# Packed fp16 splits for every attention unit, and the low parts of w_in formed by TensorE

## The chip, the cores and the metric

The kernel runs on one core of one Trainium2 chip. The metric is the device time of one execution in microseconds (us); several runs are timed and their median is used. One further execution is recorded by the hardware profiler, and its trace is what the profile below shows.

The core's engines run side by side, each through its own queue in program order: TensorE (PE; its weight loads are listed as PEld), VectorE (DVE), ScalarE (ACT), GpSimd (POOL), and SyncE (SP), which issues the transfers between HBM and on-chip memory here.

## The reference

The kernel computes an attention layer with a short window and block summaries, followed by a two-layer MLP with GELU. There are 4 batches, 8 heads, 768 positions, 64 channels a head; the MLP goes from 512 to 2048 and back, for 3072 tokens. The two weight matrices arrive as float64.

```python
k_sum = k.reshape(B, H, nb, 32, D).max(axis=3)          # 24 blocks of 32 positions
v_sum = v.reshape(B, H, nb, 32, D).mean(axis=3)
scores_l = where(|i - j| < 16, q @ k.T / 8, -1e9)
scores_s = q @ k_sum.T / 8 + log(32)
a = softmax(concat([scores_l, scores_s]))
x = (a @ concat([v, v_sum]))                              # to [3072, 512]
h = x @ w_in                                              # [3072, 2048]
out = (0.5 * h * (1 + erf(h / sqrt(2)))) @ w_out          # [3072, 512]
```

## The kernel before

**Splits.** TensorE multiplies fp16 at one pass and fp32 in several. For fp32 accuracy an operand is split into two fp16 parts, `hi = fp16(x)` and `lo = fp16(x - hi)`, and a product is three fp16 matmuls: hi by hi, hi by lo, lo by hi.

**Weights.** Each matrix is fetched in 16 pieces of 128 x 512 numbers (`fetch_w_in i`, `fetch_w_out f`). Three integer instructions on VectorE (`wi_bits i 0` to `2`, lines L294 to L303) turn float64 bits into fp32 in a buffer `wst`, of which there are three. ScalarE casts the hi part (`wi_hi`, L310), VectorE subtracts it for the lo part (`wi_lo`, L324). A piece's raw bits land in the later space of the `gh` and `gl` tiles or in a `stage` buffer.

**Attention.** The work is cut into 24 units of 4 heads by 256 queries (4 blocks of 64). For a block of 64 queries, 128 keys stand on the partitions: 64 of the window, 24 block maxima, 8 zeros, 32 of the window. A unit's steps are `load_q`, `load_k`, `load_v`, `load_vs`, then `k_hi`, `q_hi` (casts on GpSimd), `k_lo`, `q_lo` (VectorE), `scores` (TensorE, to `pss`), `add_mask` (VectorE, to `s32`), `maximum` (GpSimd, over the partitions), `shift` (VectorE), `exponent` (ScalarE), `p_hi` (GpSimd), `p_lo` (VectorE), `v_hi` (ScalarE), `v_lo` (VectorE), `values` (TensorE, to `psv`; columns of ones in v give the denominators), the norm (`norm_den` to `norm_mult`), and `x_hi`, `x_lo`. In the scores 64 rows of k's hi part and 64 rows of its lo part fill the 128 rows of the array, against q held twice, so that two matmuls (with q's hi and with its lo) make the product; q takes 1024 columns on 128 partitions, k 1280 on 64.

Units 0 to 3 (`NF = 4`, `self.fp`) take another way: mask, scores, shift and values are fp32 matmuls on data that is not split (`f_mask` L543, `scores_f` L576, `f_shift` L551 and L552, `values` L648).

**MLP.** A chunk c is 256 tokens, two units. `phase1 c i` makes 256 of the 2048 hidden columns: 24 matmuls of 256 columns (L708 to L710) into a `psh` buffer, of which there are two; it reads the w_in pieces 2i and 2i + 1. `gelu`, `g_hi` (ScalarE) and `g_lo` (VectorE) follow, over `g32` (three buffers). `phase2 c i` is 12 matmuls of 512 columns (L742 to L744) into `pso`, `store` and `put` bring a half chunk out.

**Order.** No scheduler runs: `ORDER`, a list of steps written out in the source, is walked once and each step issues its instructions, so each engine's queue and SyncE's queue of transfers have the order of that list.

Of the kernel before, what the change touches and what calls it, by code (L numbers as in the profile page):

```python
# [52 lines left out]
fill_v 0, load_k 0, fetch_vt 0, fill_v 1, fetch_k 0 1, load_mask, load_q 0, fetch_k 0 2, load_k 1, load_ind,
fetch_vt 2, prep_k 0 1, fetch_k 0 3, load_q 1, prep_k 0 2, fetch_k 0 0, fetch_w_in 10, f_mask 0, fetch_vt 1,
prep_k 0 3, load_v 0, sum_vt 0, prep_k_end 0 1, kf_sums 1, prep_k 0 0, k_sums 0 1, fetch_w_in 0, prep_k_end 0 0,
kf_sums 0, scores 0, wi_bits 10 0, fetch_w_in 4, k_sums 0 0, wi_bits 10 1, wi_bits 10 2, fetch_w_in 14, wi_hi 10,
wi_lo 10, fetch_w_in 7, sum_vt 1, f_evac 0, load_k 2, wi_bits 0 0, maximum 0, wi_bits 0 1, sum_vt 2, load_v 1,
wi_bits 0 2, wi_bits 4 0, wi_hi 0, wi_bits 4 1, f_mask 1, mean_vt, wi_bits 4 2, fetch_w_in 1, wi_lo 0, wi_hi 4,
scores 1, wi_bits 7 0, fetch_w_in 9, wi_lo 4, wi_bits 7 1, kf_sums 2, wi_bits 7 2, fetch_w_in 3, load_vs 0,
wi_bits 14 0, wi_hi 7, wi_bits 14 1, fetch_w_in 2, f_evac 1, load_vs 1, wi_lo 7, wi_bits 14 2, f_shift 0,  # L60
fetch_w_in 6, maximum 1, wi_bits 1 0, wi_hi 14, wi_bits 1 1, fetch_w_in 11, wi_bits 1 2, wi_bits 9 0, wi_hi 1,
wi_bits 9 1, fetch_w_in 8, exponent 0, wi_bits 9 2, wi_lo 1, load_q 2, wi_lo 14, fetch_w_in 5, wi_hi 9, f_shift 1,
wi_bits 3 0, wi_bits 2 0, wi_bits 2 1, fetch_w_in 12, wi_bits 2 2, wi_bits 3 1, wi_hi 2, load_k 3, wi_bits 3 2,
values 0, exponent 1, wi_lo 2, fetch_w_in 15, wi_lo 9, wi_hi 3, wi_lo 3, load_q 3, wi_bits 8 0, fetch_w_in 13,
wi_bits 5 0, wi_bits 5 1, f_mask 2, norm_den 0, wi_bits 5 2, load_v 2, wi_bits 6 0, wi_hi 5, wi_bits 8 1, scores 2,
kf_sums 3, norm_take 0, norm_rec 0, load_k 4, wi_lo 5, norm_spread 0, norm_mult 0, f_evac 2, wi_bits 6 1, values 1,
wi_bits 8 2, x_hi 0, maximum 2, wi_bits 6 2, wi_hi 8, x_lo 0, wi_hi 6, wi_lo 8, load_k 5, wi_lo 6, f_mask 3,
norm_den 1, load_v 3, wi_bits 11 0, load_vs 2, shift 2, k_hi 4, scores 3, norm_take 1, exponent 2, load_q 4,
norm_rec 1, k_hi 5, norm_spread 1, norm_mult 1, load_vs 3, load_v 4, wi_bits 11 1, x_hi 1, values 2, wi_bits 11 2,
f_evac 3, q_hi 4, x_lo 1, wi_hi 11, wi_bits 12 0, maximum 3, wi_lo 11, wi_bits 12 1, load_v 5, wi_bits 12 2,  # L70
phase1 0 0, norm_den 2, wi_bits 15 0, fetch_w_out 0, wi_bits 15 1, wi_bits 15 2, load_vs 4, wi_hi 12, norm_take 2,
wi_hi 15, fetch_w_out 6, phase1 0 1, norm_rec 2, gelu 0 0, norm_spread 2, load_vs 5, norm_mult 2, g_hi 0 0, wi_lo 12,
phase1 0 2, x_hi 2, g_lo 0 0, gelu 0 1, x_lo 2, g_hi 0 1, v_hi 4, wi_lo 15, phase1 0 3, shift 3, gelu 0 2, g_hi 0 2,
wi_bits 13 0, load_q 5, exponent 3, wi_bits 13 1, phase1 0 7, wo_bits 0 0, wo_bits 0 1, wi_bits 13 2, gelu 0 3,
wo_bits 6 0, fetch_w_out 10, wo_bits 6 1, values 3, wo_bits 6 2, wi_hi 13, g_hi 0 3, wi_lo 13, wo_hi 6, wo_bits 0 2,
v_hi 5, g_lo 0 2, fetch_w_out 1, fetch_w_out 2, wo_hi 0, g_lo 0 1, phase1 0 6, norm_den 3, wo_lo 6, wo_lo 0, gelu 0 7,
norm_take 3, g_hi 0 7, norm_rec 3, phase1 0 4, norm_spread 3, gelu 0 6, wo_bits 1 0, g_hi 0 6, norm_mult 3,
phase1 0 5, wo_bits 2 0, x_hi 3, wo_bits 1 1, x_lo 3, wo_bits 1 2, wo_bits 2 1, wo_hi 1, wo_bits 2 2, wo_lo 1,
wo_hi 2, g_lo 0 3, wo_lo 2, gelu 0 5, wo_bits 10 0, g_hi 0 5, g_lo 0 7, g_lo 0 5, gelu 0 4, g_lo 0 6, g_hi 0 4,
phase1 1 1, wo_bits 10 1, wo_bits 10 2, k_lo 4, wo_hi 10, fetch_w_out 3, fetch_w_out 4, fetch_w_out 11, wo_lo 10,  # L80
q_lo 4, load_k 6, phase1 1 2, gelu 1 1, g_lo 0 4, g_hi 1 1, wo_bits 3 0, wo_bits 3 1, wo_bits 3 2, phase1 1 3,
gelu 1 2, wo_bits 4 0, fetch_w_out 5, wo_hi 3, wo_bits 4 1, g_hi 1 2, wo_lo 3, wo_bits 4 2, phase1 1 0, gelu 1 3,
wo_bits 11 0, fetch_w_out 7, g_hi 1 3, wo_bits 11 1, wo_hi 4, wo_bits 11 2, wo_lo 4, wo_hi 11, fetch_w_out 13,
phase1 1 5, wo_bits 5 0, wo_bits 5 1, wo_bits 5 2, wo_bits 7 0, wo_hi 5, fetch_w_out 9, scores 4, wo_bits 7 1,
phase2 0 0, wo_lo 5, q_hi 5, wo_bits 7 2, k_hi 6, wo_lo 11, wo_hi 7, fetch_w_out 8, g_lo 1 1, phase2 0 1,
wo_bits 13 0, gelu 1 0, wo_bits 13 1, g_hi 1 0, wo_bits 13 2, g_lo 1 0, wo_hi 13, fetch_w_out 12, phase1 1 4, wo_lo 7,
wo_bits 9 0, wo_bits 9 1, wo_lo 13, phase2 0 2, wo_bits 8 0, wo_bits 8 1, wo_bits 9 2, wo_bits 8 2, wo_hi 9,
fetch_w_out 14, phase2 0 3, wo_bits 12 0, wo_hi 8, fetch_w_out 15, wo_lo 9, wo_lo 8, g_lo 1 3, phase2 0 5,
wo_bits 12 1, wo_bits 12 2, wo_bits 14 0, wo_hi 12, fetch_k 1 1, wo_bits 14 1, phase2 0 4, wo_bits 15 0, wo_bits 15 1,
wo_bits 14 2, wo_bits 15 2, wo_hi 14, fetch_k 1 2, wo_lo 12, wo_hi 15, fetch_k 1 0, wo_lo 14, wo_lo 15, add_mask 4,  # L90
phase2 0 7, g_lo 1 2, maximum 4, k_lo 6, gelu 1 5, g_hi 1 5, phase2 0 6, gelu 1 4, k_lo 5, g_hi 1 4, store 0 1,
g_lo 1 4, load_k 7, phase1 1 7, put 0 1, shift 4, q_lo 5, exponent 4, load_q 6, phase1 1 6, g_lo 1 5, load_k 8,
v_lo 4, gelu 1 7, p_hi 4, prep_k 1 1, load_v 6, scores 5, p_lo 4, fetch_k 1 3, gelu 1 6, q_hi 6, g_hi 1 6, add_mask 5,
values 4, g_hi 1 7, k_hi 7, store 0 0, g_lo 1 7, put 0 0, phase2 1 1, norm_den 4, maximum 5, q_lo 6, norm_take 4,
prep_k 1 0, phase2 1 3, g_lo 1 6, shift 5, phase2 1 5, v_lo 5, exponent 5, load_q 7, k_lo 7, load_v 7, phase2 1 0,
p_hi 5, prep_k_end 1 0, load_k 9, norm_rec 4, k_sums 1 0, p_lo 5, phase2 1 2, norm_spread 4, norm_mult 4, prep_k 1 2,
x_hi 4, values 5, x_lo 4, fetch_v 1 0, fetch_v 1 1, prep_k 1 3, scores 6, norm_den 5, prep_k_end 1 1, fetch_v 1 3,
phase2 1 7, q_hi 7, add_mask 6, k_sums 1 1, k_hi 8, norm_take 5, phase2 1 4, maximum 6, store 1 1, norm_rec 5,
norm_spread 5, put 1 1, norm_mult 5, q_lo 7, phase2 1 6, x_hi 5, shift 6, x_lo 5, scores 7, exponent 6, load_q 8,
prep_v 1 0, phase1 2 2, store 1 0, k_hi 9, add_mask 7, put 1 0, fetch_v 1 2, p_hi 6, prep_v 1 1, phase1 2 1, gelu 2 2,  # L100
maximum 7, p_lo 6, fetch_k 2 2, k_lo 8, g_hi 2 2, phase1 2 0, gelu 2 1, g_lo 2 2, g_hi 2 1, load_k 10, q_hi 8,
prep_v 1 2, prep_v 1 3, phase1 2 3, gelu 2 0, g_hi 2 0, shift 7, load_vs 6, g_lo 2 0, phase1 2 4, exponent 7,
load_vs 7, q_lo 8, g_lo 2 1, load_q 9, gelu 2 3, p_hi 7, scores 8, fetch_k 2 3, k_lo 9, fetch_k 2 1, phase2 2 1,
k_hi 10, p_lo 7, v_hi 6, load_k 11, v_hi 7, v_lo 6, phase2 2 0, q_hi 9, gelu 2 4, v_lo 7, load_v 8, g_hi 2 4,
g_hi 2 3, add_mask 8, values 6, g_lo 2 3, maximum 8, q_lo 9, phase1 2 6, norm_den 6, load_vs 8, g_lo 2 4, norm_take 6,
norm_rec 6, load_v 9, norm_spread 6, phase1 2 5, gelu 2 6, norm_mult 6, g_hi 2 6, shift 8, v_hi 8, values 7, x_hi 6,
g_lo 2 6, load_q 10, exponent 8, load_vs 9, phase2 2 3, x_lo 6, v_lo 8, k_lo 10, norm_den 7, load_v 10, p_hi 8,
phase2 2 2, gelu 2 5, prep_k 2 3, load_k 12, norm_take 7, norm_rec 7, phase1 2 7, v_hi 9, norm_spread 7, norm_mult 7,
load_vs 10, g_hi 2 5, g_lo 2 5, x_hi 7, scores 9, p_lo 8, gelu 2 7, g_hi 2 7, phase2 2 4, q_hi 10, x_lo 7, k_hi 11,
add_mask 9, v_lo 9, phase1 3 0, maximum 9, g_lo 2 7, load_v 11, q_lo 10, phase1 3 2, gelu 3 0, k_lo 11, g_hi 3 0,  # L110
shift 9, load_k 13, phase1 3 5, gelu 3 2, load_vs 11, g_hi 3 2, g_lo 3 0, exponent 9, g_lo 3 2, load_q 11, prep_k 2 1,
# [742 lines left out]
```

## Time and profile before

| what | us |
|---|---|
| median of 3 runs (680.51 to 684.58) | 683.58 |
| the profiled execution's own time | 686.86 |
| its span, first to last instruction | 684.8 |
| PE busy | 638.6 (93%) |
| DVE busy | 472.6 (69%) |
| ACT busy | 297.0 (43%) |
| POOL busy | 172.7 (25%) |

A page of the profile gives busy time by engine, the span in 40 slices (each digit a busy share in tenths; PEclk the clock that TensorE was granted), and groups of instructions by line. A group's row reads: line, engine, operation, out<-in by the program's tile names, sizes, count | busy us, mean ns of one | idle time of the engine just before them, and who ended it. Matmuls are pipelined, so their listed durations overlap; what one costs is the distance from its start to the next one's start. Other views used are the chain of work that ended last in order of time, the busy time of each engine in chosen stretches, the waits (who waited for whom), and the timeline.

### The profile page before, as it was taken

What the parts mean: (1) busy time and instruction counts of PE and PEld (TensorE: products, weight loads), DVE (VectorE), ACT (ScalarE), POOL (GpSimd) and SP (SyncE); (2) the same over time, 40 slices, a digit from 0 to 9 for tenths busy, and PEclk for the clock granted to TensorE, in tenths of its full rate; (3) what the DMA queues carried; (4) which work ended last, traced back from release to release, by engine and by line L of the source; (5) the groups of instructions that cost most, each with busy time, mean ns of one, the idle gap of its engine ahead of it and who ended that gap; (6) DMA issues with size and microseconds to landing.
All of it is one profiled execution on the core that took longest, in us unless ns stands there. A gap on an engine that the chain in (4) does not pass through costs nothing.

```text
span 684.8 us, 12436 instructions
## 1 busy us (share of the span) xinstructions
PE 638.6 (93%) x5356; PEld 444.2 (65%) x5356; DVE 472.6 (69%) x581; ACT 297.0 (43%) x419; POOL 172.7 (25%) x103
## 2 busy tenths in 40 slices
PE   1989999889898799999899989999999899999997
...
DVE  1784778999999998948889986628318974146210
...
PEclk9855569999999999999999999999999999999999
...
GB/s 247 378 218 199 139 66 125 149 180 152 162 117 141 167 91 225 180 57 72 91 127 79 88 77 53 133 1 111 45 16 66 84 69 16 1 32 1 16 16 32
DMA packets 26998, 72.24 MB, mean 105 GB/s; under 512 B 3008, under 2 KB 6720, under 8 KB 26944
## 3 DMA queue, kind: packets, MB, share of 16 engines
...
q8 instruction: 42, 0.69, 0.4%
...
## 4 chain that ended last, share of the span: by engine, by line
PE 66%; DVE 25%; issue 3%; DMA 2%; ACT 2%; POOL 1%; SPq 1%; DVEq 0%; ACTq 0%; POOLq 0%
PE psh L708 9%; PE psh L709 9%; PE psh L710 9%; PE pso L743 8%; PE pso L742 8%; PE pso L744 8%; PE psv L648 4%; DVE ql L568 3%; DVE gl L728 3%; PE pss L576 3%; DVE k L562 2%; DVE s L607 2%; DVE s L593 2%; PE pss L543 2%; DVE v_lo L634 2%
## 5 line engine op out<-in xcount | busy, mean ns | idle before, releaser
L708 PE MATMUL psh<-xh,w_in_h 128*128 128x256 f16 x768 | 210.4, 274 | 6.4 <-ACT g L715 6.4
L709 PE MATMUL psh<-xl,w_in_h 128*128 128x256 f16 x768 | 210.3, 274 | 0.5 <-DVE xl L698 0.5
L710 PE MATMUL psh<-xh,w_in_l 128*128 128x256 f16 x768 | 210.4, 274 | 0.0
L728 DVE SCALAR_TENSOR_TENSOR gl<-g,gh 128x512 f16<-128x512 f32 x96 | 76.7, 804 | 106.9 <-ACT gh L724 106.3
L743 PE MATMUL pso<-w_out_l,gh 128*128 128x512 f16 x384 | 146.4, 381 | 0.5 <-DVE w_out_l L324 0.5
L742 PE MATMUL pso<-w_out_h,gh 128*128 128x512 f16 x384 | 146.5, 382 | 0.0
L744 PE MATMUL pso<-w_out_h,gl 128*128 128x512 f16 x384 | 146.0, 380 | 0.0
L602 POOL PARTITION_ALL_REDUCE q<-s x24 | 82.5, 3439 | 95.9 <-ACT s L547 55.1
L715 ACT ACTIVATE g<-psh 128x512 f32<-128x512 f32 x96 | 56.9, 595 | 109.8 <-PE psh L710 107.9
L559 POOL CAST qh<-q 128x1024 f16<-128x1024 f32 x20 | 25.6, 1278 | 268.7 <-PE pss L589 254.7
L709 PEld LDWEIGHTS <-w_in_h 128*128 128x128 f16 x768 | 75.6, 98 | 18.8 <-issue 7.3
L708 PEld LDWEIGHTS <-w_in_h 128*128 128x128 f16 x768 | 75.7, 99 | 11.9
L710 PEld LDWEIGHTS <-w_in_l 128*128 128x128 f16 x768 | 75.5, 98 | 10.0 <-issue 0.9
L744 PEld LDWEIGHTS <-gl 128*128 128x128 f16 x384 | 37.8, 98 | 46.6 <-issue 1.9
L742 PEld LDWEIGHTS <-gh 128*128 128x128 f16 x384 | 37.8, 99 | 41.0 <-issue 0.8
L743 PEld LDWEIGHTS <-gh 128*128 128x128 f16 x384 | 37.8, 98 | 40.7 <-issue 0.5
L724 ACT ACTIVATE gh<-g 128x512 f16<-128x512 f32 x96 | 59.9, 629 | 2.7
L617 POOL CAST ph<-s 128x1024 f16<-128x1024 f32 x20 | 27.2, 1359 | 68.0 <-ACT s L613 68.0
L613 ACT ACTIVATE s<-s 128x1024 f32<-128x1024 f32 x22 | 23.3, 1057 | 48.5 <-DVE s L607 48.4
L651 PE MATMUL psv<-pl,v_hi 128*128 128x64 f16 x320 | 32.9, 199 | 7.6 <-DVE pl L621 7.6
L568 DVE TENSOR_TENSOR ql<-q,qh 128x1024 f16<-128x1024 f32 x20 | 39.3, 1966 | 0.1
L650 PE MATMUL psv<-ph,v_hi 128*128 128x64 f16 x320 | 33.2, 199 | 6.3 <-DVE den L680 5.9
...
## 6 DMA issues: line engine op xcount, KB each, us to landing
...
```

Source lines behind the costliest of these rows:

```text
L568: nc.vector.tensor_tensor(out=self.ql, in0=self.q32, in1=self.qh, op=ALU.subtract)
L602: nc.gpsimd.partition_all_reduce(out_ap=self.m32, in_ap=self.s32, channels=P, reduce_op=bass_isa.ReduceOp.max)
L650: nc.tensor.matmul(self.psv[:, sl], vh[:, vo : vo + P], self.ph[:, sl], start=True, stop=False)
L708: nc.tensor.matmul(ph[:, e, :], w_in_h[:, k, fs], xh[:, k, :], start=(k == 0), stop=False)
L709: nc.tensor.matmul(ph[:, e, :], w_in_h[:, k, fs], xl[:, k, :], start=False, stop=False)
L710: nc.tensor.matmul(ph[:, e, :], w_in_l[:, k, fs], xh[:, k, :], start=False, stop=(k == NCC - 1))
L715: nc.scalar.activation(g32, pht.pop((c, i)), AF.Gelu, scale=1.0 / (SC_X * SC_WI))
L724: nc.scalar.activation(gh, g32t[c, i], AF.Copy, scale=SC_G)
L728: nc.vector.scalar_tensor_tensor(out=gl, in0=g32t.pop((c, i)), scalar=SC_G, in1=gh, op0=ALU.mult, op1=ALU.subtract)
L742: nc.tensor.matmul(p, gh[:, f, js], w_out_h[:, f, :], start=(f == 0), stop=False)
L743: nc.tensor.matmul(p, gh[:, f, js], w_out_l[:, f, :], start=False, stop=False)
L744: nc.tensor.matmul(p, gl[:, f, js], w_out_h[:, f, :], start=False, stop=(f == NFC - 1))
```

## The change

1. The fp32 way of units 0 to 3 is removed, with its inputs `kf` and `vf`, the masks by matmul and the shift by matmul. All 24 units use the split path.
2. q and k are packed: two heads of a pair on the upper and the lower 64 partitions. q takes 512 columns on 128 partitions (before 1024, held twice), k 640 (before 1280 on 64). k's hi and lo parts have tiles of their own, `k_hi` and `k_lo`, in place of `k16`.
3. The scores become 48 matmuls of 64 columns on 64 rows each (before 32 on 128 rows): three products, each for the lower half of the rows (`e = 0`) and the upper half (`e = 1`) in turn, the halves to different PSUM banks.
4. The maximum goes to a tile of its own, `m32` (one buffer), not over `q32`.
5. Each w_in piece gets a `wi_diff`: TensorE forms 128 times the fp32 piece minus the hi part in a `psh` buffer (one fp32 matmul and one fp16 matmul), and ScalarE evacuates it as the lo part (`wi_lo`). w_out keeps its lo parts on VectorE.
6. `prep_k_end` writes one packed hi and lo of the block maxima (two VectorE instructions instead of five), and `k_sums` copies both with ScalarE.
7. `qh` and `ql` get two buffers each instead of one, `g32` five instead of three.
8. `ORDER` is a new list. Pieces 2, 0, 3, 1 of w_in come first and the first `phase1` stands behind 17 of the 48 `wi_bits` (before: 42).

Steps ahead of `phase1 3 0` in the two lists, where they differ or matter here:

| step | before | after |
|---|---|---|
| phase1, phase2, values, norms | 24, 21, 8, 8 | 24, 21, 8, 8 |
| scores, add_mask, shift | 10, 6, 7 | 9, 9, 9 |
| k_lo, q_lo | 7, 6 | 11, 11 |
| v_lo, p_lo | 6, 5 | 10, 8 |
| prep_k, prep_k_end | 9, 4 | 11, 5 |
| maximum | 9 | 9 |
| wi_lo on VectorE | 16 | 0 |
| wi_diff | 0 | 16 |
| wi_bits, wo_bits, wo_lo, g_lo | 48, 48, 16, 23 | 48, 48, 16, 23 |

The new list around the first `phase1`:

```diff
+load_vs 3, norm_mult 1, k_hi 5, v_hi 3, add_mask 3, q_hi 5, x_hi 1, wi_bits 4 2, x_lo 1, wi_hi 4, fetch_w_in 8,
+wi_bits 5 1, phase1 0 0, wi_bits 5 2, wi_bits 6 0, wi_hi 5, fetch_w_in 9, wi_bits 6 1, shift 2, wi_bits 6 2,
+exponent 2, maximum 3, v_lo 3, fetch_w_in 10, wi_hi 6, phase1 0 1, gelu 0 0, v_lo 2, k_lo 4, load_v 4, p_hi 2,
+g_hi 0 0, wi_diff 4, shift 3, load_k 6, gelu 0 1, wi_lo 4, wi_diff 5, wi_bits 7 0, exponent 3, wi_bits 7 1, wi_diff 6,
...
```

The core of the rest:

```diff
-    NQ16, NG32, NOT = 1, 3, 1
+    NQ16, NG32, NOT = 2, 5, 1
...
     def prep_k_end(b, g):
...
+        hi, lo = ks16[b, g][:, 0], ks16[b, g][:, 1]
+        nc.vector.tensor_copy(out=hi, in_=ks32[b][:, rs])
+        nc.vector.tensor_tensor(out=lo, in0=ks32[b][:, rs], in1=hi, op=ALU.subtract)
...
         def load_q(self):
-            self.q32 = ld.tile([P, UCOLS], F32, tag="q32", name=f"q32_{self.nm}")
-            rows = slice(0, D if self.fp else P)
-            nc.sync.dma_start(out=self.q32[rows], in_=qd[self.u, rows])
+            self.q32 = ld.tile([P, QCOLS], F32, tag="q32", name=f"q32_{self.nm}")
+            nc.sync.dma_start(out=self.q32, in_=qd[self.u])
...
+        def k_hi(self):
+            nc.gpsimd.tensor_copy(out=self.kh[:, :, 0:TQ], in_=self.k32)
...
+        def k_lo(self):
+            nc.vector.tensor_tensor(out=self.kl[:, :, 0:TQ], in0=self.k32, in1=self.kh[:, :, 0:TQ], op=ALU.subtract)
...
         def scores(self):
-            if self.fp:
-                return self.scores_f()
...
-                    nc.tensor.matmul(self.pss[:, sl], kf[:, kb : kb + P], self.qh[:, sl], start=True, stop=False)
-                    nc.tensor.matmul(self.pss[:, sl], kf[:, kb : kb + P], self.ql[:, sl], start=False, stop=True)
+            for i in range(NR * CT):
+                kb = (i // CT * (CT + 1) + i % CT) * KW
+                sl = slice(i * TQ, (i + 1) * TQ)
+                for n, (k, q) in enumerate(((kh, self.qh), (kh, self.ql), (kl, self.qh))):
+                    for e in range(2):
+                        rows = slice(e * D, (e + 1) * D)
+                        nc.tensor.matmul(
+                            self.pss[:, e * QCOLS + i * TQ : e * QCOLS + (i + 1) * TQ], k[rows, kb : kb + P], q[rows, sl],
+                            start=(n == 0 and not masked), stop=(n == 2 and (i == NR * CT - 1 or not masked)),
+                        )
...
         def maximum(self):
-            self.m32 = self.q32
+            self.m32 = wk.tile([P, UCOLS], F32, tag="m32", bufs=1, name=f"m32_{self.nm}")
```

`wi_diff i` and `load_neg` stood in the source before, uncalled; the new list calls them. `eye` is 128 times the identity, `neg` minus the identity in fp16:

```python
def weight_diff(key, dst_h):
    ps = diffs[key] = ps_h.tile([P, 2, CH], F32, tag="psh", name=f"psw_{key}")
    flat = ps.rearrange("p e j -> p (e j)")
    nc.tensor.matmul(flat, eye, raws[key], start=True, stop=False)
    nc.tensor.matmul(flat, neg, dst_h, start=False, stop=True)
```

and `weight_lo`, where such a difference exists, evacuates it on ScalarE: `nc.scalar.activation(dst_l, flat.rearrange(...), AF.Copy)`.

More of the change, by code (lines that the diff above doesn't have):

```diff
@@ L49 @@
 UPB = len(UNITS) // B
-NF = 4
 ORDER = '''
[L53 to L111, printed above, removed]
-phase1 3 1, prep_k 2 2, gelu 3 5, p_hi 9, prep_k_end 2 1, fetch_k 2 0, fetch_v 2 2, fetch_v 2 0, p_lo 9, phase2 2 6,
@@ new lines @@
+phase2 0 5, add_mask 4, k_hi 6, q_hi 6, wo_lo 12, maximum 4, g_lo 1 2, phase2 0 6, k_lo 5, q_lo 5, load_k 7, g_lo 1 1,
+load_q 7, v_lo 4, gelu 1 5, scores 5, g_hi 1 5, phase2 0 7, shift 4, store 0 0, load_v 6, put 0 0, add_mask 5,
+exponent 4, k_hi 7, q_hi 7, g_lo 1 3, phase2 1 0, maximum 5, g_lo 1 4, v_lo 5, gelu 1 7, phase2 1 2, prep_k 1 1,
+load_v 7, g_hi 1 7, g_lo 1 5, p_hi 4, store 0 1, shift 5, put 0 1, phase2 1 1, p_lo 4, exponent 5, prep_k 1 0,
+prep_k_end 1 0, phase2 1 3, fetch_k 1 2, p_hi 5, k_lo 7, k_sums 1 0, k_lo 6, p_lo 5, load_k 8, values 4, q_lo 6,
```

398 lines of the change are left out of this document (199 added, 199 removed).

## The prediction

> **What bounds the kernel now.** I read the page's slices first, then the chain of work that ended last over the first 100 us, then busy time by stretch.
>
> ```profile
> PE   1989999889898799999899989999999899999997
> DVE  1784778999999998948889986628318974146210
> PEclk9855569999999999999999999999999999999999
> ```
>
> One digit is 17.1 us. PE looks full nearly throughout, but from the third to the sixth slice its granted clock is 0.5 to 0.6, and VectorE (DVE) is full from there to slice 15 only. So there are three stages. The chain, in order of time (start us, us, what), tells what the first one is:
>
> ```profile
> 25.49 6.25 PE pso_vt L440 x8
> ...
> 38.28 2.07 PE pss L551 x2
> ...
> 55.62 7.02 PE psv L648 x32
> ...
> 87.65 7.02 PE psv L648 x32
> ```
>
> These are the fp32 matmuls of units 0 to 3: the shift by the maximum (L551 and, alike, L552; 1.0 us a record), the scores (L576), the values (L648, 7.02/32 = 0.22 us a record of 64 columns; an fp32 matmul has two records). They run one behind another at half clock until the first `phase1` can start. The stretches show the second stage:
>
> ```profile
> 0.00:95.00 95.00, 78.34 (x271) 51.43 (x272) 57.88 (x84) 24.70 (x39) 27.92 (x26) 0.68 0.68 218
> 95.00:120.00 25.00, 25.00 (x213) 22.01 (x212) 20.64 (x35) 20.30 (x29) 0.00 (x0) 0.92 0.34 109
> 120.00:250.00 130.00, 113.94 (x1036) 77.37 (x1034) 127.83 (x158) 60.52 (x85) 42.95 (x23) 0.97 0.49 149
> 250.00:685.00 435.00, 421.29 (x3844) 293.40 (x3841) 266.29 (x307) 191.46 (x267) 101.86 (x55) 1.00 0.22 68
> ```
>
> Columns: length, then busy PE, weight loads, DVE, ACT, POOL, then clock, DMA share, GB/s. From 120 to 250 us DVE is busy 127.83 of 130 and PE idles 16: DVE bounds. After 250 us PE is busy 421 of 435, and DVE 266: PE bounds, at full clock.
>
> The boundary falls on a step that makes a good ruler, `phase1 3 0`. Ahead of it, in both order lists, stand the same 24 `phase1`, 21 `phase2` and 8 `values`. In the trace it starts at 249.74:
>
> ```profile
> 249.53 0.38 PE L744 MATMUL pso<-w_out_h,gl 128*128 128x512 f16 x1
> 249.74 0.27 PE L708 MATMUL psh<-xh,w_in_h 128*128 128x256 f16 x1
> 249.85 0.27 PE L709 MATMUL psh<-xl,w_in_h 128*128 128x256 f16 x1
> ```
>
> One phase2 matmul takes 0.21 us start to start, one of phase1 0.11. The span is thus 249.7 us to the ruler plus 435.1 behind it (684.8). Ahead of the ruler DVE is busy 57.88 + 20.64 + 127.83 less the last 0.26, so 206.1 us, and idle 43.6. The sum needs four terms: DVE's work ahead, DVE's idle ahead, PE's work behind, stalls behind.
>
> **Term 1, DVE's work ahead of the ruler.** VectorE's groups in the first 250 us (count, busy us, mean ns):
>
> ```profile
> L562 DVE TENSOR_TENSOR k<-k,k 64x1280 f16<-64x1280 f32 x7 | 14.2, 2032 | 0.2
> L324 DVE SCALAR_TENSOR_TENSOR w_in_l<-wst_i,w_in_h 128x512 f16<-128x512 f32 x16 | 12.3, 784 | 17.4 <-ACT w_in_h L310 17.3
> L634 DVE SCALAR_TENSOR_TENSOR v_lo<-v,v_hi 128x512 f16<-128x512 f32 x11 | 11.3, 1069 | 0.0
> L607 DVE TENSOR_TENSOR s<-s,q 128x1024 f32<-128x1024 f32 x7 | 9.6, 1366 | 0.0
> L568 DVE TENSOR_TENSOR ql<-q,qh 128x1024 f16<-128x1024 f32 x6 | 9.0, 1498 | 0.0
> L621 DVE TENSOR_TENSOR pl<-s,ph 128x1024 f16<-128x1024 f32 x5 | 8.7, 1735 | 0.0
> L593 DVE SCALAR_TENSOR_TENSOR s<-mask_sb,pss 128x1024 f32<-128x1024 f32 x6 | 7.3, 1216 | 0.1
> L405 DVE TENSOR_REDUCE ks<-kp 128x24 f32<-128x768 f32 x5 | 4.7, 939 | 0.1
> L419 DVE TENSOR_TENSOR ksum<-ks,ks 64x48 f16<-64x48 f32 x8 | 2.6, 329 | 0.1
> L418 DVE COPY ksum<-ks 64x48 f16<-64x48 f16 x8 | 2.2, 280 | 0.3
> L680 DVE TENSOR_TENSOR den<-psv,dent 64x512 f32<-64x512 f32 x8 | 5.6, 694 | 0.1
> L414 DVE CAST ks<-ks 128x48 f16<-128x48 f32 x4 | 0.7, 187 | 0.1
> L303 DVE SCALAR_TENSOR_TENSOR wst_o<-wraw,wst_o 128x512 int32<-128x512 int32 x16 | 11.6, 733 | 0.3
> ```
>
> Counts are those of the two order lists ahead of the ruler; the packed tiles have half the columns, so I take half a row.
> - `wi_lo` leaves DVE: 16 x 0.784 = -12.5.
> - `k_lo`: 7 x 2.032 becomes 11 x 1.016: -3.0. `q_lo`: 6 x 1.498 becomes 11 x 0.749: -0.8.
> - `prep_k_end`: 4 x (0.187 + 2 x 0.280 + 2 x 0.329) becomes 5 x (0.187 + 0.329): -3.0.
> - Units 0 to 3 now use the split path. `add_mask` 6 to 9: +3.6. `shift` 7 to 9: +2.7. `v_lo` 6 to 10, two instructions each: +8.6. `p_lo` 5 to 8: +5.2. `prep_k` 9 to 11: +1.9.
>
> Sum +2.7: 208.8 us. The change takes no DVE work from the stage that DVE bounds; it gives back all it saves.
>
> **Term 2, DVE's idle time ahead of the ruler**, 43.6 us now. Who it waited for in the first 250 us (us, times, longest):
>
> ```profile
> DVE w_in_l L324 <- ACT w_in_h L310: 17.3, 5, 7.4
> DVE ks L405 <- DMA gl<-in_kp_dram: 12.2, 2, 8.3
> DVE dent L663 <- ACT den L659: 3.9, 4, 3.0
> DVE ks L405 <- DMA gh<-in_kp_dram: 3.0, 1, 3.0
> ```
>
> The 17.3 us stand on `wi_lo`, which DVE no longer has; behind them ACT, in order, was held by PE's fp32 scores. Both go. The k blocks (8.3 us to the first, 6.9 for the later ones) are fetched first instead of third, and unit 0's q and k right behind them: I take 6.5 to the first and 1 more. New waits: a unit's chain (scores, mask, maximum, shift, exponent, `p_hi`) has steps on PE, POOL and ACT, of which one is long:
>
> ```profile
> L602 POOL PARTITION_ALL_REDUCE q<-s x24 | 82.5, 3439 | 95.9 <-ACT s L547 55.1 <-DVE s L593 37.3 <-issue 3.4
> ```
>
> DVE has the integer steps of `w_in` to lay between, but none before the first piece has landed, so unit 0 and 1 cost about 7, and I leave 5.5 for the rest, nearest to the 6.6 us that it idles from 95 to 250 now. Together 20. The ends are 12 (start and a third of the rest) and 43.6 (as now). The ruler then starts at 208.8 + 20 = 228.8 instead of 249.7: -20.9.
>
> **Is PE ready for that?** Ahead of the first `phase1` the new list has, for DVE, 17 integer steps of 0.73, four each of `prep_k`, `k_lo`, `q_lo` and `add_mask`, two each of `shift`, `p_lo` and `v_lo` (38.6 us by the rows), and for each of two units the norm with `x_lo`, six instructions at most like L680's 0.69 (8.3): 47 us. With the 14.5 us of idle that lie early it starts near 62 instead of behind the last L648 of the chain, at 94.7. PE's work from there to the ruler: 24 phase1 of 24 x 0.11 = 63, 21 phase2 of 12 x 0.21 = 53, six `values` and five `scores` of 1.4 to 1.7 each, 16, and twelve `wi_diff`. One of these is two fp32 records of 512 columns, at most 6.25/8 = 0.78 each by the chain's row at mixed clock, and an fp16 one of 0.21: 1.8 x 12 = 21. Together 153 in 167 us: hidden. If that cover were gone they would cost their 21. `wi_lo` on ACT adds 16 evacuations of `psh`, of which one takes
>
> ```profile
> L715 ACT ACTIVATE g<-psh 128x512 f32<-128x512 f32 x24 | 14.1, 594 | 8.3 <-PE psh L710 6.7 <-DVE gl L728 1.5
> ```
>
> 0.6 us, to an engine busy 45 of its first 120 us: hidden, 9.5 us if not. GpSimd's casts of q and k halve, and nine maxima stay nine. The single `m32` buffer makes a maximum wait for the shift before it; on SyncE's queue `q32` comes free at `q_lo` already, and q's loads halve where DMA is not the limit (share 0.22 behind the ruler). I cost these at nothing; without cover each would show as one maximum, 3.4 us, where the next unit is late.
>
> **Term 3, PE's work behind the ruler.** 72 phase1, 75 phase2 and 16 values stand there in both lists; scores are 14 and 15. A unit's scores now, first and last matmul and what follows:
>
> ```profile
> 137.40 0.19 PE L588 MATMUL pss<-qh,k 128*128 128x64 f16 x1
> 137.43 0.19 PE L589 MATMUL pss<-ql,k 128*128 128x64 f16 x1
> 138.30 0.19 PE L589 MATMUL pss<-ql,k 128*128 128x64 f16 x1
> 138.33 0.38 PE L742 MATMUL pso<-w_out_h,gh 128*128 128x512 f16 x1
> ```
>
> 32 in 0.93 us: 0.029 each. After the change there are 48, on 64 rows each, upper and lower half in turn. No row shows two halves at once. Bounds: 0.029 each as they come (1.39), or 0.029 a pair if the halves run together (0.70). I take the single one, the nearest row in type and width. And changing between 64 and 128 rows has a price that the fp32 scores show:
>
> ```profile
> 24.65 0.84 PE L576 MATMUL pss<-q,w_out_h 64*128 64x64 f32 x3
> 25.08 0.42 PE L576 MATMUL pss<-q,w_out_h 64*128 64x64 f32 x1
> 25.43 1.15 PE L440 MATMUL pso_vt<-vt,ind_sb 128*88 128x512 f32 x1
> ```
>
> Three starts to 25.08 are 0.215 apart, the next, on 128 rows, comes 0.35 later: 0.135 lost. The Trainium skill, "TensorEngine Tiling (Array Packing)", section Key Properties, says that changing the tiling mode drains the engine while changing the tile alone does not; the row agrees with the first half, and no row here shows the second. Twice 0.135 a unit: 15 x (1.39 + 0.27) - 14 x 0.93 = +11.9. In pairs it would be 15 x (0.70 + 0.27) - 14 x 0.93 = +1.5.
>
> **Term 4, stalls behind the ruler.** PE idles 13.7 of 435 us there, the tail among it. DVE's work behind the ruler falls by 24 us (13 `k_lo` by 1.016 each, and `q_lo` from 14 x 1.498 to 13 x 0.749), so its late results, which are what PE waits for, come earlier: I take -4; ends 0 and -9.
>
> **Sum:** -20.9 + 11.9 - 4 = -13.0. Against the profiled execution, 686.86 us (span 684.8 and 2.1 around it): 673.9. That execution lies 3.3 above the median of the three runs shown, 683.58, to which the comparison will be made: 670.6, so 671.
>
> **The rivals.**
> - The halves run in pairs: term 3 is +1.5, the time 660. For it: two halves write different PSUM banks and alternate. Against: each matmul here already starts every 0.029 us with a weight load of its own, so the start may be the limit and not the columns. Chance 0.28. The Trainium skill, "TensorE: Matmul & The Clock Gate", Part 3, has matmuls on different row groups run at once; by that rule this case comes out. Its Part 1 has no two starts closer than about 25 ns, and by that figure term 3 would be an estimated +9.0. No row here shows either.
> - Idle moves instead of going. `wst` has three buffers; now `wi_bits` of a piece must wait for `wi_diff` three pieces back, which stands in PE's queue behind a `phase1` of 2.6 us and needs a `psh` buffer that ACT must empty first. Behind a waiting `wi_bits` stand, on DVE, the norms and `g_lo` that PE wants. Twelve pieces waiting 2 us each are 24 us; idle is 44 again and the time 695, slower. It decides at 33 us of idle (no gain) and 40 (over 1% lost). Against it: between `phase1 0 1` and `0 7` the new list has 37 integer steps, 27 us, and about 15 of other DVE work, 7 per pair of pieces, and PE has 2.6 + 2 x 1.8 = 6.2 for a pair. Chance 0.12.
> - Half of that, idle 28 to 33: 679 to 684, within 1%. Chance 0.15.
> - My forecast: 0.45.
>
> About 1% is what a measurement of this kernel can tell from no change. Faster by more, under 676.7: the pairs, and nine tenths of the forecast's 0.45: 0.68. Within: 0.20. Slower: 0.12. The range goes from 653 (the pairs with idle near 13) to 687 (idle near 36), and leaves out most of the slow rival.
>
> **What would show it.** The first `phase1` near 62 us and the ruler near 229; DVE busy about 209 ahead of it; no granted clock of 0.5 beyond some 60 us; scores of 1.4 us plus 0.13 at each end; no wait of `wst` on PE over 1 us. I am wrong if the ruler starts after 241 (no gain), or if 48 score matmuls take under 1 us or over 2.5.

## The result, and the profile after

| | before | after |
|---|---|---|
| median of 4 runs each, us | 682.61 | 650.60 (649.37 to 651.77) |
| ratio, with its 95% interval | 1 | 0.953 (0.950 to 0.957) |
| profiled execution, its own time, us | 686.86 | 651.77 |
| its span, us | 684.8 | 649.5 |

The changed kernel is faster, 32 us, where 13 were forecast. 651 lies below the range of 653 to 687. The sign held, and so did what bounds each stage; the price of the scores did not, and the two terms ahead of the ruler, the start of `phase1 3 0`, were too large as well. The slices of the profile after, one digit for 16.2 us, answer to those of before:

```profile
PE   3457799799899998998899999999999999999997
DVE  6999989989999879249966296939518473543100
PEclk9666999999999998999999999999999999999999
```

The granted clock is low in slices 2 to 4 only (before, in slices 2 to 6), and VectorE is busy for 80% or more of every slice from the second to the fourteenth, in which the ruler lies. The ruler is the second row here, in the timeline of TensorE (start us, duration us, instruction):

```profile
217.82 0.38 PE L709 MATMUL pso<-w_out_h,gl 128*128 128x512 f16 x1
218.04 0.27 PE L673 MATMUL psh<-xh,w_in_h 128*128 128x256 f16 x1
```

It stood at 249.74, so 31.7 us of the gain lie ahead of it. The stretches, with the columns that those of before have:

```profile
0.00:62.00 62.00, 32.48 (x341) 18.10 (x342) 54.16 (x63) 20.44 (x31) 32.69 (x35) 0.74 0.71 256
62.00:120.00 58.00, 50.03 (x400) 34.37 (x399) 55.17 (x87) 38.08 (x61) 7.99 (x5) 0.99 0.45 146
120.00:218.04 98.04, 93.09 (x967) 61.17 (x966) 93.06 (x129) 53.02 (x75) 33.07 (x20) 1.00 0.51 159
218.04:650.00 431.96, 421.49 (x4117) 289.89 (x4115) 240.47 (x292) 192.13 (x271) 92.12 (x56) 1.00 0.20 59
```

Ahead of the ruler VectorE is busy 54.16 + 55.17 + 93.06 = 202.4 us and idle 218.0 - 202.4 = 15.6. Behind it, PE is busy 421.5, as before (421.3 from 250.00 on), of 431.5 us to the span's end (435.0 before). With the four terms of the prediction:

| term | forecast | measured | off by |
|---|---|---|---|
| 1: VectorE's work ahead of the ruler | 208.8 | 202.4 | -6.4 |
| 2: VectorE's idle time ahead | 20 | 15.6 | -4.4 |
| 3 and 4: the stretch behind, against 435.0 | +11.9 - 4 = +7.9 | -3.5 | -11.4 |
| profiled execution | 673.9 | 651.77 | -22.1 |

Half of the miss is one term. A unit's scores, first and last records and what stands around them, show it. TensorE's timeline lists two matmuls of a pair as one row (x2); a start-to-start distance between rows is thus a pair's:

```profile
141.47 0.38 PE L709 MATMUL pso<-w_out_h,gl 128*128 128x512 f16 x1
141.79 0.20 PE L554 MATMUL pss<-qh,k_hi 64*128 64x64 f16 x2
141.82 0.19 PE L554 MATMUL pss<-ql,k_hi 64*128 64x64 f16 x2
...
142.44 0.19 PE L554 MATMUL pss<-ql,k_hi 64*128 64x64 f16 x2
142.47 0.19 PE L554 MATMUL pss<-qh,k_lo 64*128 64x64 f16 x2
142.59 0.39 PE L707 MATMUL pso<-w_out_h,gh 128*128 128x512 f16 x1
```

The 24 pairs start between 141.79 and 142.47, so one follows another after 0.68/23 = 0.030 us: a pair costs what the prediction gave a single matmul. 48 score matmuls take under 1 us, which the prediction named as a sign that it is wrong. On either side the change between 128 and 64 rows shows: 0.32 from the last 512-column matmul to the first score instead of the usual 0.21, and 0.12 from the last score to the next matmul instead of 0.03, so some 0.1 at each end. A unit costs 142.59 - 141.47 - 0.21 = 0.91 us, against 0.93 of the 32 full-array matmuls before. The 15 units behind the ruler show the same 0.68 and the same two ends, but for one whose start waits for VectorE.

### The profile page after: what moved, and what is told of

Same layout as the page of the kernel before. It is cut to its first block, busy times and chain, and to the rows that moved or that the text cites. A ratio compares the mean times of both kernels' runs of the same rounds, so it can differ in the third digit from the quotient of the medians.

```text
span 649.5 us, 13381 instructions
## 1 busy us (share of the span) xinstructions
PE 597.1 (92%) x5820; PEld 403.5 (62%) x5820; DVE 442.9 (68%) x567; ACT 303.7 (47%) x436; POOL 165.9 (26%) x115
## 4 chain that ended last, share of the span: by engine, by line
PE 63%; DVE 24%; issue 4%; DMA 4%; POOL 3%; ACT 1%; SPq 1%; DVEq 0%; POOLq 0%; ACTq 0%
PE psh L673 10%; PE psh L675 10%; PE psh L674 10%; PE pso L707 9%; PE pso L708 9%; PE pso L709 9%; DVE s L565 2%; DVE k_lo L537 2%; PE pss L554 2%; DVE v_lo L603 2%; DVE pl L590 2%; DVE s L579 1%; DVE gl L693 1%; PE psv L616 1%; PE psv L617 1%
## 5 line engine op out<-in xcount | busy, mean ns | idle before, releaser
L693 DVE SCALAR_TENSOR_TENSOR gl<-g,gh 128x512 f16<-128x512 f32 x96 | 69.6, 732 | 110.8 <-ACT gh L689 110.7
L574 POOL PARTITION_ALL_REDUCE m<-s x24 | 84.9, 3539 | 55.8 <-DVE s L565 36.0
L674 PEld LDWEIGHTS <-w_in_h 128*128 128x128 f16 x768 | 75.4, 98 | 23.3 <-issue 11.4
L530 POOL CAST k_hi<-k 128x640 f16<-128x640 f32 x24 | 21.5, 895 | 249.4 <-PE pss L554 235.3
L675 PEld LDWEIGHTS <-w_in_l 128*128 128x128 f16 x768 | 75.4, 98 | 11.2 <-issue 1.7
L616 PE MATMUL psv<-ph,v_hi 128*128 128x64 f16 x384 | 39.4, 198 | 9.5 <-DVE den L645 9.5
L616 PEld LDWEIGHTS <-v_hi 128*128 128x128 f16 x384 | 35.7, 101 | 13.2 <-issue 11.9
L586 POOL CAST ph<-s 128x1024 f16<-128x1024 f32 x24 | 31.8, 1323 | 44.2 <-ACT s L582 43.9
L617 PE MATMUL psv<-pl,v_hi 128*128 128x64 f16 x384 | 39.0, 198 | 3.8 <-DVE pl L590 3.7
L714 ACT ACTIVATE ot<-pso 128x512 f32<-128x512 f32 x24 | 14.3, 596 | 59.3 <-PE pso L709 58.7
```

The lines of the kernel that those rows point to most:

```text
L574: nc.gpsimd.partition_all_reduce(out_ap=self.m32, in_ap=self.s32, channels=P, reduce_op=bass_isa.ReduceOp.max)
L616: nc.tensor.matmul(self.psv[:, sl], vh[:, vo : vo + P], self.ph[:, sl], start=True, stop=False)
L617: nc.tensor.matmul(self.psv[:, sl], vh[:, vo : vo + P], self.pl[:, sl], start=False, stop=False)
L674: nc.tensor.matmul(ph[:, e, :], w_in_h[:, k, fs], xl[:, k, :], start=False, stop=False)
L675: nc.tensor.matmul(ph[:, e, :], w_in_l[:, k, fs], xh[:, k, :], start=False, stop=(k == NCC - 1))
L693: nc.vector.scalar_tensor_tensor(out=gl, in0=g32t.pop((c, i)), scalar=SC_G, in1=gh, op0=ALU.mult, op1=ALU.subtract)
```

## The experiments

Each kernel was timed beside the kernel before; "ratio" is to that kernel's time, with its 95% interval. Lines of the order list are shortened to the steps that differ. For reading them side by side, here are the ruler and what lies on its two sides in each profiled execution (us; ahead = VectorE's time ahead of the ruler, behind = from the ruler to the span's end):

| kernel | first `phase1` | ruler | ahead: busy | ahead: idle | behind |
|---|---|---|---|---|---|
| before | 94.5 | 249.7 | 206.1 | 43.6 | 435.0 |
| after | 52.8 | 218.0 | 202.4 | 15.6 | 431.5 |
| halves apart, in after | 54.8 | 220.7 | 202.3 | 18.4 | 434.8 |
| lo parts on VectorE, in after | 52.7 | 225.5 | 211.9 | 13.5 | 428.0 |
| `wi_diff` in before | 95.6 | 255.8 | 194.6 | 61.2 | 435.8 |
| no fp32 units in before | 103.1 | 263.5 | 241.6 | 21.9 | 435.0 |
| lo subtractions twice, in after | 56.6 | 236.7 | 218.5 | 18.1 | 430.7 |
| all three undone, in after | 60.3 | 244.0 | 227.1 | 16.9 | 434.8 |
| w_out differences, in after | 53.0 | 225.0 | 198.2 | 26.8 | 427.9 |
| casts of q and k on ScalarE | 51.8 | 216.0 | 199.5 | 16.5 | 428.3 |
| casts of q, k, p on ScalarE | 50.3 | 211.5 | 194.8 | 16.6 | 426.9 |
| the same, in all units | 48.8 | 211.6 | 194.9 | 16.7 | 425.4 |
| casts and copies of v on ScalarE | 51.7 | 213.8 | 190.7 | 23.1 | 426.9 |

**Do the halves run in pairs?** The same matmuls, all of the lower half and then all of the upper:

```diff
-            for i in range(NR * CT):
+            for e, i in ((e, i) for e in range(2) for i in range(NR * CT)):
...
-                    for e in range(2):
```

> The changed kernel with one edit: all score matmuls of the lower row half are issued first, then all of the upper half, so that two halves never stand next to each other (once a unit apart). Theory A, the two halves run at the same time when they alternate: here a unit's 48 matmuls start 0.029 us apart, 1.39 us instead of 0.68; 15 units behind phase1 3 0 cost 15 x 0.70 = 10.5 us, the nine ahead of it, where VectorE bounds, 0 to 6 more: 661 to 667 us. Theory B, a matmul on 64 rows is simply half as long by itself: scores stay at 0.68 us and the time at 651.

Measured: 657.76, ratio 0.963 (0.960 to 0.966), so 7.2 us above after. TensorE's timeline of this kernel at a unit's scores:

```profile
142.35 0.38 PE L709 MATMUL pso<-w_out_h,gl 128*128 128x512 f16 x1
142.66 0.20 PE L554 MATMUL pss<-qh,k_hi 64*128 64x64 f16 x1
142.70 0.19 PE L554 MATMUL pss<-ql,k_hi 64*128 64x64 f16 x1
...
143.22 0.19 PE L554 MATMUL pss<-ql,k_hi 64*128 64x64 f16 x1
143.25 0.19 PE L554 MATMUL pss<-qh,k_lo 64*128 64x64 f16 x1
143.26 0.21 PE L554 MATMUL pss<-qh,k_hi 64*128 64x64 f16 x2
143.30 0.20 PE L554 MATMUL pss<-ql,k_hi 64*128 64x64 f16 x2
143.33 0.20 PE L554 MATMUL pss<-qh,k_lo 64*128 64x64 f16 x2
143.36 0.19 PE L554 MATMUL pss<-qh,k_hi 64*128 64x64 f16 x1
...
143.94 0.19 PE L554 MATMUL pss<-qh,k_lo 64*128 64x64 f16 x1
144.06 0.39 PE L707 MATMUL pso<-w_out_h,gh 128*128 128x512 f16 x1
```

48 matmuls now start over 1.28 us, 0.027 each on average: within a half one starts every 0.029 us (x1). The halves meet once, from 143.26 on, and there alone the last three of one run beside the first three of the other (x2). The pairs are what makes the scores cheap, and they depend on the order of issue: neighbours on different row halves run at once, neighbours on the same half do not. Each half also writes to a PSUM bank of its own, in after as here, so no run changes the rows alone. That the banks by themselves do it is unlikely: in the kernel before, 64-column matmuls on all 128 rows go from `psv` (192.82) to `pss` (192.85) without starting closer than 0.029 us, and so they do where the scores pass from the first 512 columns of `pss` to the last.

The time rose by less than the 15 x 0.6 = 9 us that the scores behind the ruler take more, and by less than the 661 to 667 us expected: in the profiled executions by 3.3 us behind the ruler and 2.7 ahead. Behind it PE is busy 428.3 us, 6.8 more than in after, whose execution has 3.4 us at a granted clock of 0.5 there, from 254.5 us on, which this one has not; PE's gaps, added up from its records, fell from 6.2 to 2.7 us. So part of the longer scores filled waits that PE had anyway.

**Was it right to take the lo parts of w_in off VectorE?** In the new list each `wi_diff i` is replaced by `wi_lo i`, which then goes back to VectorE:

```diff
-fetch_w_in 7, wi_hi 2, wi_bits 0 2, wi_diff 2, wi_bits 3 0, wi_hi 0, load_vs 0, fetch_w_in 6, shift 1, wi_diff 0,
+fetch_w_in 7, wi_hi 2, wi_bits 0 2, wi_lo 2, wi_bits 3 0, wi_hi 0, load_vs 0, fetch_w_in 6, shift 1, wi_lo 0,
...
```

> The changed kernel with wi_lo back on VectorE, at the places where wi_diff stood; wi_diff is gone from TensorE. Theory A, VectorE's queue sets the time ahead of phase1 3 0 (202.4 us busy of 218.0): it gets 16 x 0.69 to 0.78 = 11 to 12.5 us more and a few waits for wi_hi, the step starts at 229 to 233 and the time is 662 to 667. Theory B, TensorE bounds there too and the gain came from elsewhere: TensorE loses 16 x 1.07 = 17 us, the time stays at 651 or falls.

Measured: 656.04, ratio 0.960 (0.957 to 0.963), 5.4 us above after. VectorE has these instructions more, ahead of the ruler:

```profile
L324 DVE SCALAR_TENSOR_TENSOR w_in_l<-wst_i,w_in_h 128x512 f16<-128x512 f32 x16 | 13.6, 851 | 0.0
```

Its busy time there grows by 9.5 us, since its other instructions take 4.1 less, and its idle time falls by 2.1; the ruler moves by 7.4. The stretch behind it is 3.5 shorter, of which the 3.4 us at half clock in after's execution account for some 1.7. The move to TensorE helps, but by less than half of the 13.6 us of VectorE's work; the time lies between those of the two theories.

**The same move alone, in the kernel before**, whose list has the fp32 units in front:

```diff
-load_k 1, load_ind,
+load_k 1, load_ind, load_neg,
...
-fetch_w_in 14, wi_hi 10, wi_lo 10,
+fetch_w_in 14, wi_hi 10, wi_diff 10, wi_lo 10,
...
```

> The kernel before with the change's wi_diff alone: every wi_lo gets a wi_diff on TensorE and is evacuated by ScalarE. Theory A, its first 95 us are a chain on TensorE at half clock: 13 differences of 1.1 to 1.9 us stand in that chain, the first phase1 moves from 94.5 to about 110, and since VectorE is idle there anyway its 12.5 us are worth little: 690 to 700 us. Theory B, taking wi_lo from VectorE is worth its 12.5 us in either kernel: 670 us.

Measured: 694.85, ratio 1.017 (1.014 to 1.020): slower by 12 us (the two profiled executions are 6.9 us apart, as that of the kernel before lies 4 above its median). VectorE's waits in the first 255 us (us, times, longest):

```profile
DVE wst_i L296 <- PE psw_i L317: 14.2, 5, 9.8
DVE ks L407 <- DMA gl<-in_kp_dram: 12.0, 2, 7.9
DVE dent L665 <- ACT den L661: 9.4, 4, 5.6
```

VectorE is busy 11.5 us less ahead of the ruler and idle 17.6 more. The first line is the prediction's slower rival: `wst` comes free when PE has read it. What PE does before the end of the longest of these waits, at 58.9 us, is in its timeline:

```profile
47.91 1.12 PE L553 MATMUL pss<-s,ind_sb 128*128 128x512 f32 x2
48.97 1.12 PE L554 MATMUL pss<-q,w_out_l 1*128 1x512 f32 x2
50.02 6.95 PE L650 MATMUL psv<-s,w_out_l 128*128 128x64 f32 x32
56.76 2.02 PE L317 MATMUL psw_i<-wst_i,ind_sb 128*128 128x512 f32 x2
```

`wi_diff` (L317) stands in PE's queue behind a unit's fp32 shift and values. In after, VectorE's waits ahead of the ruler are

```profile
DVE ks L418 <- DMA gl<-in_kp_dram: 3.8, 1, 3.8
DVE s L565 <- PE pss L554: 2.2, 2, 1.2
DVE ks L418 <- DMA gh<-in_kp_dram: 1.6, 2, 1.2
...
DVE wst_i L287 <- PE psw_i L316: 0.6, 1, 0.6
...
DVE wst_o L287 <- PE psw_i L316: 0.4, 1, 0.4
```

and that wait is 1.0 us in all. The same move is worth -5.4 us in one list and +12 in the other.

**No fp32 units, alone.** In the kernel before, units 0 to 3 take the split path that its other units have, with wide operands; their steps stand where the fp32 steps stood:

```diff
-            self.fp = u < NF
+            self.fp = False
...
-kf_sums 0, scores 0,
+k_sums 0 0, k_hi 0, q_hi 0, k_lo 0, q_lo 0, scores 0,
...
```

> The kernel before with the fp32 way of units 0 to 3 taken out and nothing else: those units use its own split path (1024 columns of q, 128-row scores), their steps at the places of the fp32 steps in its order list. Theory A, removing fp32 pays only with the packed tiles and the new order: VectorE gets four units of 8.6 us and two shifts, 37 us more ahead of phase1 3 0, and loses at most 20 to 30 of its 43.6 us of idle; the step starts at 258 to 268 instead of 249.7 and the time is 692 to 702. Theory B, the fp32 chain at half clock was the loss and its end the gain: the first phase1 starts near 65 instead of 94.5 and the time is 655 to 668.

Measured: 698.98, ratio 1.023 (1.020 to 1.026): slower by 16 us. The stretch to the first `phase1` and the one up to 250 us:

```profile
0.00:103.00 103.00, 24.58 (x283) 17.27 (x284) 86.00 (x104) 22.16 (x30) 37.78 (x35) 0.65 0.56 191
103.00:250.00 147.00, 128.57 (x1156) 90.92 (x1154) 142.45 (x182) 72.88 (x104) 44.66 (x23) 0.94 0.46 142
```

PE is busy only 24.58 of the first 103 us, but the first `phase1` comes at 103.1, later than before: with the fp32 matmuls gone, VectorE (86.0 of 103) is what it waits for most, 27.7 us for `k_lo` and 16.9 for `p_lo`. The idle time does go, from 43.6 to 21.9, as the prediction had it; the subtractions, masks and shifts of four more units, 35.5 us of VectorE's work ahead of the ruler, more than fill it.

**What the packing is worth.** In after, `k_lo` and `q_lo` of the units ahead of the ruler are issued twice, which gives VectorE about the work of the wide operands:

```diff
-            nc.vector.tensor_tensor(out=self.ql, in0=self.q32, in1=self.qh, op=ALU.subtract)
+            for _ in range(2 if self.u < 11 else 1):
+                nc.vector.tensor_tensor(out=self.ql, in0=self.q32, in1=self.qh, op=ALU.subtract)
...
```

> The changed kernel with k_lo and q_lo of units 0 to 10 issued twice on VectorE (the second writes the same values), which puts back what the packed tiles halved. Theory A, the packed tiles carry most of what turns the loss of e4_split_in_before (699 us) into the gain: VectorE gets 11 x 1.28 + 11 x 0.77 = 22 us more ahead of phase1 3 0, the step starts at 236 to 240 instead of 218 and the time is 668 to 673. Theory B, the new order list carries it: VectorE's queue has room and the time stays within 4 us of 651.

Measured: 669.49, ratio 0.982 (0.975 to 0.990), 18.9 us above after. VectorE ahead of the ruler:

```profile
L538 DVE TENSOR_TENSOR k_lo<-k,k_hi 128x640 f16<-128x640 f32 x22 | 22.4, 1026 | 1.4 <-POOL k_hi L530 1.0
L543 DVE TENSOR_TENSOR ql<-q,qh 128x512 f16<-128x512 f32 x20 | 13.7, 687 | 0.3
```

16.1 us of work more ahead of the ruler, 18.6 us later. Work on VectorE in this stage costs about its full length.

**Do the parts add up?** Three of the edits to after at once: halves apart, lo parts of w_in on VectorE, subtractions twice.

> The changed kernel with the edits of e1_halves_apart, e2_lo_on_dve and e5_lo_twice together: row halves apart, wi_lo on VectorE, k_lo and q_lo of units 0 to 10 issued twice. What is left of the change against e4_split_in_before (699 us) is the new order list with its buffers and the shorter prep_k_end. Theory A, VectorE's queue sets the time ahead of phase1 3 0, so the three add up there: 7 + 5 + 19 = 31 us above 651, 678 to 685, and the new list is worth 14 to 21 us by itself. Theory B, they hide behind one another: 669 to 675, the list worth over 24. Theory C, each was hiding another's cost: over 690, the list worth nothing.

Measured: 682.20, ratio 1.002 (0.998 to 1.005): the time of the kernel before. 5.4 + 7.2 + 18.9 = 31.5, measured 31.6. So the balance of the change reads, in us: removing the fp32 units +16.4 (in the old list), the VectorE work that packing saves ahead of the ruler -18.9, halves in pairs -7.2, lo parts of w_in on TensorE and ScalarE -5.4, and for all the rest 682.2 - 699.0 = -16.8. That rest is the new list with its buffers, the shorter `prep_k_end`, and what packing saves elsewhere (half of q's and k's transfers and casts, and VectorE's work of units 11 to 23). How the 16.8 are shared was not tried.

**Further along the same line: the low parts of w_out.** `wo_diff f` is put ahead of `wo_lo f` for six of the sixteen pieces of w_out:

```diff
-wi_lo 15, fetch_w_out 3, wo_lo 0,
+wi_lo 15, wo_diff 0, fetch_w_out 3, wo_lo 0,
...
```

> The changed kernel with the lo parts of six pieces of w_out (0, 2, 1, 3, 8, 11) formed by TensorE and ScalarE like those of w_in. Theory A, VectorE still sets the time ahead of phase1 3 0: it loses 6 x 0.69 = 4.1 us, the step starts at 214 to 216, the time is 647 to 649. Theory B, TensorE, busy 93 of the 98 us before that step, is as much the bound: its 6 x 1.07 = 6.4 us more eat the gain, the time is 651 to 656.

Measured: 655.01, ratio 0.962 (0.954 to 0.971), 4.4 us above after. VectorE's longest wait ahead of the ruler is now

```profile
DVE wst_o L289 <- PE psw_o L318: 8.9, 3, 6.1
```

It is busy 4.2 us less and idle 11.2 more: the prediction's slower rival again, at the spot where PE, busy 101 of the 105 us from 120 us to the ruler, is full too.

**Is VectorE slowed by GpSimd?** Term 1 was off by 6.4 us although the counts were right (to one `q_lo`). VectorE's rows in after, ahead of the ruler, against those of before that the prediction used:

```profile
L603 DVE SCALAR_TENSOR_TENSOR v_lo<-v,v_hi 128x512 f16<-128x512 f32 x20 | 15.6, 829 | 0.0
L537 DVE TENSOR_TENSOR k_lo<-k,k_hi 128x640 f16<-128x640 f32 x11 | 14.0, 1283 | 0.0
L590 DVE TENSOR_TENSOR pl<-s,ph 128x1024 f16<-128x1024 f32 x8 | 10.6, 1322 | 0.9 <-POOL ph L586 0.9
```

`v_lo` has the same shape as before and takes 829 ns instead of 1069, `p_lo` 1322 instead of 1735. Two instances of `k_lo` and GpSimd's instructions around them, from the timelines of the two engines:

```profile
14.05 2.51 DVE L537 TENSOR_TENSOR k_lo<-k,k_hi 128x640 f16<-128x640 f32 x1
66.46 0.81 DVE L537 TENSOR_TENSOR k_lo<-k,k_hi 128x640 f16<-128x640 f32 x1
```

```profile
13.98 3.23 POOL L574 PARTITION_ALL_REDUCE m<-s  x1
...
64.56 1.44 POOL L586 CAST ph<-s 128x1024 f16<-128x1024 f32 x1
68.67 1.03 POOL L512 COPY v<-w_out_l 24x1024 f32<-24x1024 f32 x1 [2.68 <-DMA v<-in_vw_dram]
```

The first `k_lo` lies within a maximum and takes three times as long as the second, which runs while GpSimd idles. Adding up what each of VectorE's instructions takes over the shortest of its kind gives 26 us ahead of the ruler in after and 35 in before. Where it lies shows in the records: of the 276 instructions there in after, 190 run beside no instruction of GpSimd, and none of these is over 0.15 us longer than the shortest of its kind, though the DMA engines are more than half busy during 113 of them; the 86 others hold all but 1 us of the 26. In before it is the same: 207 beside none, and 68 that hold all but 2 us of the 35. So the transfers are not the cause. If it is GpSimd's doing, casts moved from GpSimd to ScalarE shorten VectorE's work without touching it. First those of q and k, units 0 to 10:

```diff
         def k_hi(self):
+            if self.u < NACT:
+                nc.scalar.activation(self.kh[:, :, 0:TQ], self.k32, AF.Copy)
+                return
             nc.gpsimd.tensor_copy(out=self.kh[:, :, 0:TQ], in_=self.k32)
...
```

> As e6_casts_on_act, but k_hi and q_hi alone go to ScalarE; p_hi stays on GpSimd. Theory A: about half of e6's fall in VectorE's busy time, 2 to 6 us, the time 645 to 650. Theory B: 650 to 657.

Measured: 645.86, ratio 0.948 (0.941 to 0.955). Then `p_hi` too:

> The changed kernel with k_hi, q_hi and p_hi of units 0 to 10 on ScalarE instead of GpSimd; GpSimd keeps the maxima. In the trace of the changed kernel VectorE's instructions ahead of phase1 3 0 take 26 us more than as many of the shortest of their kind, and the long ones stand beside GpSimd's work. Theory A, GpSimd's casts stretch them: VectorE's busy time ahead of the step falls from 202.4 by 5 to 10 us, the step starts at 208 to 214 and the time is 641 to 648. Theory B, the stretch comes from the maxima or ScalarE's queue becomes late: VectorE's busy time falls by under 3 us, the time is 650 to 660.

Measured: 640.63, ratio 0.940 (0.933 to 0.947). VectorE ahead of the ruler:

```profile
L613 DVE SCALAR_TENSOR_TENSOR v_lo<-v,v_hi 128x512 f16<-128x512 f32 x20 | 15.2, 809 | 1.1 <-ACT v_hi L607 1.0
L544 DVE TENSOR_TENSOR k_lo<-k,k_hi 128x640 f16<-128x640 f32 x11 | 11.4, 1054 | 0.9 <-ACT k_hi L532 0.9
```

VectorE has the same 567 instructions, and its busy time ahead of the ruler falls from 202.4 to 194.8; its idle time rises by 1.0 only. Then in all 24 units (`NACT = 24`):

> As e6_casts_on_act (641 us), for all 24 units. Behind phase1 3 0 TensorE bounds and VectorE has room, so its shorter instructions are worth at most the 5 us of stalls left there: 637 to 641 us. Rival: ScalarE, which also evacuates psh for TensorE, becomes late behind the step: 642 to 650.

Measured: 638.37, ratio 0.937 (0.930 to 0.945), the best of all kernels here, 12 us under the changed kernel. Last, with units 0 to 10, the copies of `load_vs` in batch 0 as well:

```diff
-                nc.gpsimd.tensor_copy(out=dst, in_=means)
+                nc.scalar.activation(dst, means, AF.Copy)
```

> As e6_casts_on_act (641 us), with the six copies of the value means of batch 0 (load_vs) moved from GpSimd to ScalarE as well. They stand beside VectorE's work early: 1 to 3 us less of VectorE's busy time, 638 to 641 us. Rival: ScalarE's queue delays v_hi and the evacuations early on: 641 to 646.

Measured: 643.33, ratio 0.945 (0.939 to 0.951), worse than without. VectorE is busy 4.1 us less still, but idle 6.5 more; its longest wait ahead of the ruler is new:

```profile
DVE v_lo L613 <- ACT v_hi L607: 4.2, 3, 2.4
```

ScalarE, in order, now brings `v_hi` late.

## Why the prediction was right or wrong

**What bounds, right.** VectorE bounds up to the ruler and PE behind it, before and after. The experiments on VectorE's work moved the ruler by about as much (16.1 more, 18.6 later; 9.5 more, 7.4 later).

**Term 1, mis-sized by 6.4 us.** The counts were right to one `q_lo`; the durations came from rows of before that contain the delay by GpSimd. "`v_lo` 6 to 10, two instructions each: +8.6" was 15.6 - 11.3 = +4.3 (20 records in place of 11), and "`p_lo` 5 to 8: +5.2" was 10.6 - 8.7 = +1.9. The other way, "11 x 1.016" for `k_lo` was 11 x 1.283, since four of the eleven start beside a maximum or a cast of GpSimd and take 1.66 to 2.51. "It gives back all it saves" held nearly: 206.1 before, 202.4 after.

**Term 2, mis-sized by 4.4.** The idle time goes as forecast, with the first k block at 3.8 us and not 6.5, and `add_mask` waiting 2.2 us for scores in two places, where 7 had been put for the chains of units 0 and 1. That removing the fp32 units takes the idle time away was right; removed alone it makes the kernel slower, which the prediction's sum contains (its +22.0 for units 0 to 3) but does not say.

**Is PE ready, right.** First `phase1` at 52.8 (62 forecast). Its matmuls wait twice for x, 3.4 us together, and follow each other from 57.5 on, 0.21 us apart at a granted clock of 0.5 and 0.11 from 63.2 on, where the low clock ends; no `wst` waited over 1 us on PE.

**Term 3, the step that failed.** "I take the single one, the nearest row in type and width": 0.029 us for each of 48 matmuls. The rows quoted had one width and one mode; between the two bounds given, 0.029 each and 0.029 a pair, they could not decide, and the argument against the pairs (that the start is the limit) is what the kernel with the halves apart refutes: 0.029 us each on one half, 0.030 a pair when in turn. With 0.1 instead of 0.135 for each change between 64 and 128 rows (the 0.135 came from an fp32 row at half clock) the term is 15 x 0.91 - 14 x 0.93 = +0.6 and not +11.9. This was the rival that the halves run in pairs, with a chance of 0.28 and +1.5. The Trainium skill, "TensorE: Matmul & The Clock Gate", Part 3, has matmuls on different row groups start about 4 ns apart; the trace agrees, with 2 to 5 ns between the starts within a pair. The same page's Part 1 has no two starts closer than about 25 ns; that agrees with 29 ns on one half and does not hold between halves.

**Term 4, right in size, and half right in cause.** With +0.6 for the scores, 3.5 us less behind the ruler leaves -4.1; -4 was forecast. PE's gaps, added up from the records, fell by 3.5, from 9.7 to 6.2: its waits for VectorE, which the prediction named, from 7.9 to 6.2, and one wait of 1.8 for `gelu` on ScalarE is gone, which it did not. Each of the two executions has one stretch of 3.4 us at half clock behind the ruler (331.2 us, 254.5 us), so that drops out.

**The rivals of the other side.** Waits of `wst` on PE came to 1.0 us in this list. They are real: 14.2 us in the kernel before with `wi_diff`, 8.9 with `wo_diff`. In both, PE had no room where VectorE needed the buffer back.

Had the pairs and their change of mode been taken as measured, the sum would have come to about 673.9 - 11.3 = 662.6 for the profiled execution; the rest, 10.8 us, is terms 1 and 2.
